# Talking-heads attention and a feed-forward layer: score tiles of 8 heads x 16 queries, and feed-forward work queued between the chunks of the next batch

## The chip, the cores and the metric

The kernel runs on one core of one Trainium2 chip. The metric is the device time of one execution in microseconds (us). "PE" is TensorE's matmul stream, "PEld" its weight loads, DVE is VectorE, ACT ScalarE, POOL GpSimd. PSUM is the memory that matmuls write, in eight banks that this kernel gives out through pools.

## The reference, cut to what matters

There are 8 batches of 12 heads, 448 positions and 64 columns a head. All inputs are float32, and the kernel computes in bfloat16 with float32 accumulation.

```python
scores = (1 / 8) * (q @ k.transpose(0, 1, 3, 2))            # [8, 12, 448, 448]
scores = einsum('bhij,hg->bgij', scores, w_pre)              # mix the heads
attn   = softmax(scores, axis=-1)
attn   = einsum('bhij,hg->bgij', attn, w_post)               # mix them again
x      = (attn @ v) as 3584 rows of 768
out    = maximum(x @ w_in, 0) ** 2 @ w_out                   # 768 -> 2048 -> 768
```

Mixing heads is a matmul over the partition axis if the partitions of a score tile hold (head, query) pairs. One tile holds 128 of the 12 x 448 pairs.

## The kernel before

A batch is 14 chunks of 32 queries. A chunk has three score tiles, each of 4 heads x 32 queries, made by two 64-column matmuls (two heads each). Every output tile of the first mixing needs all three, so mixing is 3 x 3 matmuls of 448 columns. The second mixing and the transposition of the weights come together: the normalised tile is the stationary operand and a matrix built from `w_post` is the moving one, 4 row blocks x 3 matmuls of 384 columns.

```python
for b in range(B):
    ...                                                   # cut: loads of batch b + 1
    for c in range(NCH + 1):
        if c < NCH:
            for t in range(3):                            # scores, 2 x 64 columns
                s_ps = psA.tile(...)
                for x in range(2):
                    nc.tensor.matmul(s_ps[64*x:64*x+64, 0:S], lhsT=ql[2*t+x][:, c, :], rhs=kt[2*t+x], ...)
                # copied to bfloat16 by ScalarE (t < 2) or VectorE
            for gqo in range(3):                          # mixing: 3 x 3 matmuls
                for t in range(3):
                    nc.tensor.matmul(m_ps, lhsT=wpre_cat[t][:, gqo*128:(gqo+1)*128], rhs=S_t[t], ...)
                nc.scalar.activation(e_sb, m_ps, Exp, scale=SCALE, accum_out=sm)
                nc.vector.reciprocal(rc, sm)
                nc.vector.tensor_scalar(d_sb, e_sb, rc, 1.0 / S, mult, subtract)
        if c >= 1:
            for jb in range(4):                           # second mixing, 4 x 3 matmuls
                for t in range(3):
                    nc.tensor.matmul(at_ps[0:jsize, 0:384], lhsT=Dprev[t][:, 128*jb:...], rhs=wpost_cat[t], ...)
                nc.vector.tensor_copy(atb[jb][0:jsize, :, C32(c - 1)], at_ps[0:jsize, 0:384])
    # the mean that was subtracted comes back as a bias: column sums of v, by matmuls
    # ot = v.T @ at, then the first feed-forward (16 x 6 matmuls), transposes of batch b + 1,
    # the second feed-forward (8 blocks x 16 matmuls)                    # cut
```

The softmax here doesn't subtract the row's maximum and nothing guards it: scores larger than these inputs give would overflow.

Of the kernel before, what the change touches and what calls it, by code (L numbers as in the profile page):

```python
# [9 lines left out]
F32 = mybir.dt.float32  # L11

B, H, S, D = 8, 12, 448, 64
DMODEL = H * D
DFF = 2048
CH = 32
NCH = S // CH
ST = [128, 128, 128, 64]
NST = 4
NPAIR = H // 2  # L20
NQ = H // 4
FT = DFF // 128
SCALE = 1.0 / 8.0
ACT = mybir.ActivationFunctionType
ALU = mybir.AluOpType


def C32(cc):
    return slice(cc * CH, (cc + 1) * CH)


@with_exitstack
def kernel(
# [18 lines left out]
    qlp = ctx.enter_context(tc.tile_pool(name="qlp", bufs=1))  # L52
    atbp = ctx.enter_context(tc.tile_pool(name="atbp", bufs=1))
    ffnp = ctx.enter_context(tc.tile_pool(name="ffnp", bufs=1))
    psA = ctx.enter_context(tc.tile_pool(name="psA", bufs=5, space=bass.MemoryType.PSUM))
    psB = ctx.enter_context(tc.tile_pool(name="psB", bufs=3, space=bass.MemoryType.PSUM))
# [3 lines left out]
    istripe = consts.tile([P, 32], BF16, name="istripe")  # L60
    nc.vector.tensor_add(out=istripe[:, :], in0=ident[:, 0:32], in1=ident[:, 32:64])
    nc.vector.tensor_add(out=istripe[:, :], in0=istripe[:, :], in1=ident[:, 64:96])
    nc.vector.tensor_add(out=istripe[:, :], in0=istripe[:, :], in1=ident[:, 96:128])
    onescol = consts.tile([P, 1], BF16, name="onescol")
    nc.vector.memset(onescol[:, :], 1.0)
    onescol_f = consts.tile([P, 1], F32, name="onescol_f")
    nc.vector.memset(onescol_f[:, :], 1.0)
# [3 lines left out]
    wcol_pre = []  # L71
    wcol_post = []
    for t in range(NQ):
        wpre_t = consts.tile([P, H], F32, name=f"wcolpre{t}")
        wpost_t = consts.tile([P, H], F32, name=f"wcolpost{t}")
        for hq in range(4):
            h = 4 * t + hq
            src_pre = bass.AP(tensor=w_pre.tensor, offset=w_pre[h, 0:1].offset, ap=[[0, 32], [1, H]])
            nc.sync.dma_start(out=wpre_t[32 * hq:32 * hq + 32, 0:H], in_=src_pre)
            src_post = bass.AP(tensor=w_post.tensor, offset=w_post[h, 0:1].offset, ap=[[0, 32], [1, H]])  # L80
            nc.sync.dma_start(out=wpost_t[32 * hq:32 * hq + 32, 0:H], in_=src_post)
        wcol_pre.append(wpre_t)
        wcol_post.append(wpost_t)

    wpre_cat = []
    wpost_cat = []
    for t in range(NQ):
        a_t = consts.tile([P, H * 32], BF16, name=f"wprecat{t}")
        b_t = consts.tile([P, H * 32], BF16, name=f"wpostcat{t}")
        for g in range(H):  # L90
            nc.vector.tensor_scalar_mul(out=a_t[:, g * 32:(g + 1) * 32], in0=istripe[:, :], scalar1=wcol_pre[t][:, g:g + 1])
            nc.vector.tensor_scalar_mul(out=b_t[:, g * 32:(g + 1) * 32], in0=istripe[:, :], scalar1=wcol_post[t][:, g:g + 1])
        wpre_cat.append(a_t)
        wpost_cat.append(b_t)
# [3 lines left out]
    cg_ps = psB.tile([P, 384], F32, name="cg_ps", tag="psB")  # L98
    nc.tensor.matmul(cg_ps[0:64, 0:H], lhsT=onesblk[0:H, 0:64], rhs=wpost_bf[0:H, 0:H], start=True, stop=True)
    nc.tensor.matmul(cg_ps[64:128, 0:H], lhsT=onesblk[0:H, 0:64], rhs=wpost_bf[0:H, 0:H], start=True, stop=True)  # L100
    cg2 = consts.tile([P, H], F32, name="cg2")
    nc.vector.tensor_scalar_mul(out=cg2[:, 0:H], in0=cg_ps[:, 0:H], scalar1=1.0 / S)
    cgblk = consts.tile([P, NPAIR], F32, name="cgblk")
    for c2 in range(NPAIR):
        nc.vector.tensor_copy(out=cgblk[0:64, c2:c2 + 1], in_=cg2[0:64, 2 * c2:2 * c2 + 1])
        nc.vector.tensor_copy(out=cgblk[64:128, c2:c2 + 1], in_=cg2[64:128, 2 * c2 + 1:2 * c2 + 2])

    ql = []
    for p in range(NPAIR):
        ql_p = qlp.tile([P, NCH, 64], BF16, name=f"ql{p}", tag=f"ql{p}", bufs=1)  # L110
        nc.vector.memset(ql_p[:, :, :].rearrange("p a b -> p (a b)"), 0.0)
        ql.append(ql_p)

    w1 = []
    w2 = []

    def emit_w1_loads():
        for c2 in range(NPAIR):
            w1_c = wts.tile([P, DFF], BF16, name=f"w1_{c2}")
            nc.gpsimd.dma_start(out=w1_c[:, :], in_=moe_w_in[c2 * 128:(c2 + 1) * 128, 0:DFF])  # L120
            w1.append(w1_c)

    def emit_w2_loads():
        for ft in range(FT):
            w2_f = wts.tile([P, DMODEL], BF16, name=f"w2_{ft}")
            nc.gpsimd.dma_start(out=w2_f[:, :], in_=moe_w_out[ft * 128:(ft + 1) * 128, 0:DMODEL])
            w2.append(w2_f)

    def load_stage(b):
        qs = []  # L130
        ks = []
        vs = []
        for st in range(NST):
            nrows = ST[st]
            s0 = 128 * st
            qst = stage.tile([P, H, D], BF16, name="qst", tag="qst", bufs=8)
            nc.gpsimd.dma_start(out=qst[0:nrows, :, :], in_=q[b, :, s0:s0 + nrows, :].rearrange("h s d -> s h d"))
            qs.append(qst)
            kst = stage.tile([P, H, D], BF16, name="kst", tag="kst", bufs=8)
            nc.gpsimd.dma_start(out=kst[0:nrows, :, :], in_=k[b, :, s0:s0 + nrows, :].rearrange("h s d -> s h d"))  # L140
            ks.append(kst)
            vst = stage.tile([P, H, D], BF16, name="vst", tag="vst", bufs=8)
            nc.gpsimd.dma_start(out=vst[0:nrows, :, :], in_=v[b, :, s0:s0 + nrows, :].rearrange("h s d -> s h d"))  # L143
            if st == NST - 1:
                nc.vector.memset(vst[64:128, :, :].rearrange("p h d -> p (h d)"), 0.0)
            vs.append(vst)
        return qs, ks, vs

    def emit_prologue(qs, ks):
        qt = []  # L150
        kt = []
        for p in range(NPAIR):
            qt_ps = psA.tile([P, S], BF16, name="qt_ps", tag="psA")
            for st in range(NST):
                nrows = ST[st]
                src2d = qs[st][0:nrows, :, :].rearrange("s h d -> s (h d)")
                nc.tensor.transpose(qt_ps[:, 128 * st:128 * st + nrows], src2d[:, p * 128:(p + 1) * 128], ident[0:nrows, 0:nrows])  # L157
            qt_p = work.tile([P, S], BF16, name="qt_p", tag="qt", bufs=6)
            nc.vector.tensor_copy(out=qt_p[:, :], in_=qt_ps[:, :])
            qt.append(qt_p)  # L160
            kt_ps = psA.tile([P, S], BF16, name="kt_ps", tag="psA")
            for st in range(NST):
                nrows = ST[st]
                src2d = ks[st][0:nrows, :, :].rearrange("s h d -> s (h d)")
                nc.tensor.transpose(kt_ps[:, 128 * st:128 * st + nrows], src2d[:, p * 128:(p + 1) * 128], ident[0:nrows, 0:nrows])  # L165
            kt_p = work.tile([P, S], BF16, name="kt_p", tag="kt", bufs=6)
            nc.scalar.copy(out=kt_p[:, :], in_=kt_ps[:, :])
            kt.append(kt_p)
            nc.vector.tensor_copy(out=ql[p][0:64, :, 0:32], in_=qt_p[0:64, 0:S])
            nc.vector.tensor_copy(out=ql[p][64:128, :, 32:64], in_=qt_p[64:128, 0:S])  # L170
        return qt, kt

    staged = {}
    staged[0] = load_stage(0)
    emit_w1_loads()
    staged[1] = load_stage(1)
    emit_w2_loads()
    prologued = {}
    prologued[0] = emit_prologue(staged[0][0], staged[0][1])

    for b in range(B):
        qs, ks, vs = staged[b]
        qt, kt = prologued[b]

        if 1 <= b and b + 1 < B:
            staged[b + 1] = load_stage(b + 1)

        atb = []
        for jb in range(NST):
            t_ = atbp.tile([P, H, S], BF16, name=f"atb{jb}", tag=f"atb{jb}", bufs=1)  # L190
            atb.append(t_)
        nc.gpsimd.memset(atb[NST - 1][64:128, :, :].rearrange("p h d -> p (h d)"), 0.0)

        Dprev = None
        for c in range(NCH + 1):
            if c < NCH:
                S_t = []
                for t in range(NQ):
                    s_ps = psA.tile([P, S], F32, name="s_ps", tag="psA")
                    for x in range(2):  # L200
                        p = 2 * t + x
                        nc.tensor.matmul(  # L202
                            s_ps[64 * x:64 * x + 64, 0:S],
                            lhsT=ql[p][:, c, :],
                            rhs=kt[p][:, 0:S],
                            start=True,
                            stop=True,
                        )
                    s_sb = work.tile([P, S], BF16, name="s_sb", tag="S", bufs=6)
                    if t < 2:  # L210
                        nc.scalar.copy(out=s_sb[:, :], in_=s_ps[:, :])  # L211
                    else:
# [42 lines left out]
            if c < NCH:  # L255
                Dprev = Dcur
# [98 lines left out]
```

## Time and profile before

The median of two runs was 981.12 us (980.83 to 981.42).

These are lines of the page of the kernel before: the span; busy time, share of the span and instructions of each engine; the granted TensorE clock in 40 slices, in tenths; and the chain of work that ended last, by engine.

```profile
span 979.9 us, 15128 instructions
PE 935.6 (95%) x5698; PEld 486.8 (50%) x5698; DVE 594.5 (61%) x1633; ACT 456.3 (47%) x1185; POOL 141.9 (14%) x133
PEclk9999999999999999999999999999999999999999
PE 88%; DVE 6%; ACT 4%; DMA 1%; issue 1%; SPq 1%; ACTq 0%; DVEq 0%
```

PE is busy in 95% of the span at its full clock, and the chain runs through PE for 88%. So time is saved by taking work from TensorE, not from another engine.

One batch of the kernel before in windows (each row a stretch of time, with the busy time of each engine in it, the granted clock and the DMA engines' share): chunks; bias and products with v; first feed-forward; second feed-forward with the transposes of q and k.

```profile
core 0: us, PE busy (x) PEld busy (x) DVE busy (x) ACT busy (x) POOL busy (x), PEclk, DMA share, GB/s
268.10:335.90 67.80, 65.42 (x383) 31.99 (x381) 53.67 (x153) 38.10 (x113) 0.00 (x0) 1.00 0.01 3
335.90:343.20 7.30, 7.30 (x64) 3.60 (x61) 2.13 (x5) 2.72 (x5) 0.00 (x0) 1.00 0.01 2
343.20:361.40 18.20, 18.20 (x99) 9.39 (x97) 9.39 (x16) 8.91 (x17) 8.40 (x5) 1.00 0.60 39
361.40:386.80 25.40, 25.40 (x175) 15.68 (x174) 6.96 (x20) 7.08 (x14) 7.62 (x8) 1.00 0.99 102
```

The 118.7 us of a batch are 67.8 us of chunks (14 of 4.84) and 50.9 us of the rest; PE is nearly full in each row.

Matmuls overlap, so a duration (0.35 us) is not a cost. The cost is the distance to the next start: 189 ns for 448 columns, 162 ns for 384.

### The profile page before, as it was taken

The page shows a single profiled execution, that of the slowest core. Times are in us where ns is not written, and L with a number is a line of the kernel's source. Part 1 is how long each engine was busy: PE and PEld are TensorE (multiplying, and loading weights), DVE is VectorE, ACT ScalarE, POOL GpSimd, SP SyncE. Part 2 cuts the span into 40 slices and gives each one's busy share as a digit, 9 for nine tenths or more (in the row PEclk, how much of TensorE's full clock was granted, in tenths as well). Part 3 has the DMA queues.
Part 4 walks back from the last instruction along what each step waited for, and adds up shares of the span by engine and source line. Part 5 has one row for each costly group of instructions (what it writes and reads, how often), then busy time and mean ns, then how long its engine had stood idle before and what let it go on. Part 6 is the DMA issues. An engine that isn't in the chain of part 4 may idle for free.

```text
span 979.9 us, 15128 instructions
## 1 busy us (share of the span) xinstructions
PE 935.6 (95%) x5698; PEld 486.8 (50%) x5698; DVE 594.5 (61%) x1633; ACT 456.3 (47%) x1185; POOL 141.9 (14%) x133
## 2 busy tenths in 40 slices
PE   2999999999999999999999999999999999999998
PEld 1444565445644455444554445544455444554455
DVE  7788436874178661886628855388544884358840
ACT  1555425545265452554435544355434554355441
POOL 7570330003300032001410023000300001000000
PEclk9999999999999999999999999999999999999999
DMA  9990490004900049001580045500400000100001
GB/s 133 181 171 2 29 106 9 1 1 29 109 5 1 1 29 113 1 1 8 37 98 1 1 27 44 73 1 1 29 29 28 1 1 2 41 17 1 1 1 57
DMA packets 143177, 34.83 MB, mean 36 GB/s; under 512 B 133120, under 2 KB 142336, under 8 KB 143104
## 3 DMA queue, kind: packets, MB, share of 16 engines
q0 software_dynamic: 133760, 22.81, 29.9%
q1 hardware_dynamic: 9344, 11.05, 3.5%
q8 instruction: 44, 0.72, 0.3%
q14 instruction: 29, 0.24, 0.1%
HBM read 45.65 MB, written 11.01 MB: 58 GB/s over the span
## 4 chain that ended last, share of the span: by engine, by line
PE 88%; DVE 6%; ACT 4%; DMA 1%; issue 1%; SPq 1%; ACTq 0%; DVEq 0%
PE m_ps L219 20%; PE at_ps L247 19%; PE o_ps L314 17%; PE h_ps L293 15%; PE s_ps L202 7%; PE ot_ps L278 4%; ACT e_sb L228 3%; PE kt_ps L165 2%; DVE d_sb L232 2%; PE qt_ps L157 2%; PE colsum_ps L264 1%; ACT s_sb L211 1%; DVE rc L230 1%; DMA wcolpost_108<-in_w_post_dram 1%; DMA wcolpost_118<-in_w_post_dram 0%
## 5 line engine op out<-in xcount | busy, mean ns | idle before, releaser
L228 ACT ACTIVATE e_sb<-m_ps 128x448 f32<-128x448 f32 x336 | 181.0, 542 | 172.5 <-PE m_ps L219 148.4
L247 PEld LDWEIGHTS <-d_sb 128*128 128x128 bf16 (+1 forms) x1344 | 127.7, 100 | 154.6 <-DVE d_sb L232 46.1
L247 PE MATMUL at_ps<-wpostcat_128,d_sb 128*128 128x384 bf16 x448 | 146.2, 330 | 14.5 <-DVE d_sb L232 5.8
L213 DVE CAST s_sb<-s_ps 128x448 bf16<-128x448 f32 x112 | 67.7, 605 | 137.5 <-PE s_ps L202 137.5
L232 DVE TENSOR_SCALAR d_sb<-e_sb,rc 128x448 bf16<-128x448 f32 x336 | 144.3, 453 | 1.5
L247 PE MATMUL at_ps<-wpostcat_154,d_sb 128*128 128x384 bf16 x448 | 144.6, 326 | 0.4 <-DVE d_sb L232 0.2
L211 ACT CAST s_sb<-s_ps 128x448 bf16<-128x448 f32 x224 | 116.4, 532 | 43.3 <-PE s_ps L202 24.8
L247 PE MATMUL at_ps<-wpostcat_180,d_sb 128*128 128x384 bf16 x448 | 131.1, 326 | 0.1
L301 ACT ACTIVATE hr<-h_ps 128x448 f32<-128x448 f32 x128 | 69.7, 544 | 75.7 <-PE h_ps L293 75.7
L143 POOL DMA_DIRECT2D vst<-in_v_dram x32 | 30.8, 972 | 481.4 <-PE ot_ps L278 478.0
L219 PE MATMUL m_ps<-s_sb,wprecat_127 128*128 128x448 bf16 x336 | 94.8, 354 | 5.8 <-ACT s_sb L211 5.5
L322 ACT COPY osb<-o_ps 128x384 f32<-128x384 f32 (+1 forms) x64 | 30.6, 477 | 136.3 <-PE o_ps L314 93.6
L219 PE MATMUL m_ps<-s_sb,wprecat_153 128*128 128x448 bf16 x336 | 93.0, 354 | 0.0
L219 PE MATMUL m_ps<-s_sb,wprecat_179 128*128 128x448 bf16 x336 | 87.7, 354 | 0.3 <-DVE s_sb L213 0.3
L230 DVE RECIPROCAL rc<-sm 128x1 f32<-128x1 f32 x336 | 52.6, 157 | 33.9 <-ACT e_sb L228 26.6
L228 ACT ACTIVATION_READ_ACCUMULATOR e_sb<-m_ps 128x1 f32 x336 | 66.7, 199 | 0.0
L286 ACT ACTIVATE xt_c<-ot_ps,bvec 128x448 bf16<-128x448 f32 x48 | 27.7, 634 | 57.4 <-DVE bvec L270 56.4
L219 PEld LDWEIGHTS <-wprecat_127 128*128 128x128 bf16 x336 | 30.0, 97 | 42.8 <-issue 29.4
L219 PEld LDWEIGHTS <-wprecat_153 128*128 128x128 bf16 x336 | 32.8, 98 | 29.4 <-issue 0.8
L219 PEld LDWEIGHTS <-wprecat_179 128*128 128x128 bf16 x336 | 33.0, 98 | 28.3 <-issue 1.2
L293 PE MATMUL h_ps<-xt_c,w_0_262 128*128 128x448 bf16 x128 | 45.2, 353 | 0.0
L293 PE MATMUL h_ps<-xt_c,w_3_268 128*128 128x448 bf16 x128 | 45.1, 352 | 0.0
(561 smaller groups left out, 1794.7 us busy)
## 6 DMA issues: line engine op xcount, KB each, us to landing
out_dram<-osb SPq DMA_DIRECT2D x48, 192.0 KB, 1.9
qst<-in_q_dram POOLq DMA_DIRECT2D x24, 192.0 KB, 6.1
kst<-in_k_dram POOLq DMA_DIRECT2D x24, 192.0 KB, 6.6
vst<-in_v_dram POOLq DMA_DIRECT2D x24, 192.0 KB, 5.2
out_dram<-osb SPq DMA_DIRECT2D x16, 96.0 KB, 2.1
qst<-in_q_dram POOLq DMA_DIRECT2D x8, 96.0 KB, 7.5
kst<-in_k_dram POOLq DMA_DIRECT2D x8, 96.0 KB, 7.9
vst<-in_v_dram POOLq DMA_DIRECT2D x8, 96.0 KB, 5.4
```

The costliest lines, as they stand in the source:

```text
L202: nc.tensor.matmul(s_ps[64 * x:64 * x + 64, 0:S], lhsT=ql[p][:, c, :], rhs=kt[p][:, 0:S], start=True, stop=True,)
L211: nc.scalar.copy(out=s_sb[:, :], in_=s_ps[:, :])
L213: nc.vector.tensor_copy(out=s_sb[:, :], in_=s_ps[:, :])
L219: nc.tensor.matmul(m_ps[:, 0:S], lhsT=wpre_cat[t][:, gqo * 128:(gqo + 1) * 128], rhs=S_t[t][:, 0:S], start=(t == 0), stop=(t == NQ - 1),)
L228: nc.scalar.activation(out=e_sb[:, :], in_=m_ps[:, :], func=ACT.Exp, scale=SCALE, accum_out=sm[:, 0:1])
L230: nc.vector.reciprocal(out=rc[:, 0:1], in_=sm[:, 0:1])
L232: nc.vector.tensor_scalar(out=d_sb[:, :], in0=e_sb[:, :], scalar1=rc[:, 0:1], scalar2=1.0 / S, op0=ALU.mult, op1=ALU.subtract,)
L247: nc.tensor.matmul(at_ps[0:jsize, 0:384], lhsT=Dprev[t][:, 128 * jb:128 * jb + jsize], rhs=wpost_cat[t][:, 0:384], start=(t == 0), stop=(t ...
L278: nc.tensor.matmul(ot_ps[64 * hh:64 * hh + 64, 0:S], lhsT=vs[jb][:, g, :], rhs=atb[jb][:, g, :], start=(jb == 0), stop=(jb == NST - 1),)
L293: nc.tensor.matmul(h_ps[:, 0:S], lhsT=w1[c2][:, ft * 128:(ft + 1) * 128], rhs=xt[c2][:, 0:S], start=(c2 == 0), stop=(c2 == NPAIR - 1),)
L301: nc.scalar.activation(out=hr[:, :], in_=h_ps[:, :], func=ACT.Relu)
L314: nc.tensor.matmul(o_ps[0:msize, 0:384], lhsT=h2t[ft][:, mt * 128:mt * 128 + msize], rhs=w2[ft][:, nt * 384:(nt + 1) * 384], start=(ft == ...
```

## The change

Its intent is to make the mixing denser. A score tile now holds 8 heads x 16 queries (two tiles for heads 0 to 7), and a third tile holds heads 8 to 11 of both query groups. The first two output tiles then need two matmuls each; the third needs one full matmul and two half ones of 64 columns that can run side by side. Scores are made by 32-column matmuls, four to a tile. In the second mixing, a 384-column matmul and two of 192 do what three of 384 did, and the last 64 rows of both tiles share a PSUM tile. The bias takes 24 one-column matmuls. The last 64 rows of the second feed-forward are made for both halves at once. Squares move from VectorE to GpSimd. And the products with v, the feed-forward and the next transposes go into a list of units, from which each chunk takes some.

```diff
+    def chunk_scores(b, c):
+        for t in range(3):
+            for r in range(4):                      # four 32-column matmuls a tile
+                p, n = (r, 2*c + t) if t < 2 else (4 + r % 2, 2*c + r // 2)
+                nc.tensor.matmul(ps[32*r:32*r+32, 0:S], lhsT=ql[b % 2][p][:, n, :], rhs=kt[p][:, 0:S], ...)
+    def chunk_mix(b, c):
-            for t in range(NQ): nc.tensor.matmul(m_ps, lhsT=wpre_cat[t][...], rhs=S_t[t], ...)   # 3 x 3
+        for u, A in enumerate((A0, A1)):
+            nc.tensor.matmul(ps[:, 0:S], lhsT=preA[:, 0:128], rhs=A, ...)
+            nc.tensor.matmul(ps[:, 0:S], lhsT=preBA[u], rhs=Bt, ...)
+        nc.tensor.matmul(ps[:, 0:S], lhsT=preBB, rhs=Bt, ...)
+        for u, A in enumerate((A0, A1)):
+            nc.tensor.matmul(ps[64*u:64*u+64, 0:S], lhsT=preA[:, 128:192], rhs=A, ...)
+    def chunk_post(b, c):
+        for jb in range(3):
+            nc.tensor.matmul(ps[:, 0:384], lhsT=dB[:, js], rhs=postBB, ...)
+            nc.tensor.matmul(ps[:, 0:192], lhsT=d0[:, js], rhs=postA, ...)
+            nc.tensor.matmul(ps[:, 192:384], lhsT=d1[:, js], rhs=postA, ...)
+        # last 64 rows: four 64-column matmuls of 192
...                                                 # cut: loads, constants, bias, ot, feed-forward units
+    def run_filler(ns):
+        while filler and ns > 0:
+            w, f = filler.pop(0)
+            f()
+            ns -= w
+        return ns
+    for s in range(len(steps) + 2):
+        chunk_scores(step s); chunk_mix(step s - 1); chunk_post(step s - 2)
+        # appended where due: ot_units, ffn_units, bias_unit; at the front: prologue_units
+        debt = run_filler(3200 + debt)
```

PSUM goes from pools of 5 and 3 banks to four pools of 2. In the start, the zero fills of the query tiles move from VectorE to GpSimd.

A slot is the 0.19 us from one matmul of 448 columns to the next. A mode switch is a change between output tiles of 32, 64 and 128 columns. The order in which TensorE gets its matmuls is not that of the source: a scheduler makes it when the kernel is built, and "the built order" is its result.

## The prediction

> **What bounds it now.** TensorE. The page shows PE busy 95% at a granted clock of 1.0, and the chain that ended last is 88% PE. The timeline splits a batch of 118.7 us into 67.8 us of chunks (14 of 4.84 us), 7.3 us of bias and attention-times-V, 18.2 us of first and 20.4 us of second feed-forward matmuls, 4.9 us of transposes; 27 us precede the first chunk. By starts of consecutive matmuls, 448 columns cost 189 ns and 384 cost 163 ns; 64-column output tiles run two at a time (second start about 10 ns later). Going from 128- to 64-column matmuls or back costs 285 instead of 189 ns: about 95 ns per switch. The Trainium skill (TensorEngine Tiling (Array Packing), Key Properties) says that changing the tiling mode drains TensorE; this trace agrees. Per chunk VectorE works 3.9 us, ScalarE 3.3.
>
> **What the change does per chunk.** Mixing falls from 9 to 6 slots of 189 ns, post-mixing from 12 x 163 ns to 3 x 327 plus about 165. Scores stay 3 slots only if four 32-column tiles run together; the skill (same page, Theoretical Speedup) gives "up to 4x", no trace here shows it. Without mode switches that is 2.8 us. But the built program's order has about ten switches per chunk (32 / 128 / 64 columns interleaved; a score tile is also split, costing a slot) against two to four before. I sum 3.2 us streaming + 0.95 us switching = 4.17 us, against 4.84 measured. VectorE loses one 0.54 us eviction but keeps a cast (0.60), three evictions (0.55), three normalisations (0.41), one reciprocal: 3.7 us. ScalarE gains an eviction: two casts (0.53), three exps (0.74 with accumulator read), about 0.35: 3.6 us. Walking one period by hand through the waits (third mixing tile, exp, reciprocal, normalisation, post-mixing, next third mixing tile) gives about 4.3 us; with slack 4.45.
>
> **What it does not do.** The diff issues feed-forward between chunks. In the built order each batch's 96 + 96 + 32 feed-forward matmuls stand in one unbroken block after its chunks. So chunks still run without filler, and the overlap gains nothing. What gains is the last 64 rows of the second feed-forward, two halves together (about 2.6 us per batch), and the bias (24 tiny matmuls for 8 of 384 columns). Squares move to GpSimd: estimated from the skill (GPSIMD Engine Reference, Elementwise side-by-side) at 2.6 cycles an element, about 1 us, just under the 1.13 us of a unit, so roughly hidden.
>
> **Sum.** Batch: chunks 62, transposes 5 to 6, bias 2, attention-times-V 6, feed-forward 37 to 38: about 113 us, against 118.7. Start about 22 us (V no longer sits between Q and K loads). Total about 920 us, range 885 to 960. Chances: faster by over 2% 0.89, within 2% 0.08, slower 0.03.
>
> **What would show it.** Timeline: unbroken feed-forward of 36 to 38 us per batch; chunk period 4.2 to 4.7 us; score matmuls in groups of four starting within some 10 ns of each other; switches near 95 ns. PE stays the chain's main engine; GpSimd squares near 1 us.
>
> **What would make it wrong.** Four score tiles not running together (+1 us a chunk or more: no gain or slower). A switch to 32 columns costing more than 95 ns. GpSimd squares far over 1.13 us, holding up feed-forward. Evictions with 16-element runs slower than 0.55 us. On the other side, tile queues overlapping across segments: near 4.0 us a chunk, 880 us.

## More of the kernel before

A round is up to four 32-column score matmuls side by side.

## The result, and the profile after

The median was 917.03 us (916.87 to 917.19, two runs), ratio 0.9342 with a 95% interval of 0.9315 to 0.9369. A ratio here is the mean time of one kernel's runs over that of the other's runs in the same rounds, so it is not quite the ratio of the medians quoted. The change is faster by 6.6%, and 3 us from the prediction.

The same lines of the page, after:

```profile
span 915.4 us, 17324 instructions
PE 872.0 (95%) x6914; PEld 434.1 (47%) x6914; DVE 429.8 (47%) x1070; ACT 502.3 (55%) x1337; POOL 241.9 (26%) x277
PEclk9999999999999999999999999999999999999999
PE 5%; DVE 0%; ACT 0%; issue 0%; ACTq 0%
```

PE is as full as before with 64 us less work. The chain of waits is of no use here: it breaks off after 5% of the span, so its shares say nothing about what limited the rest. The windows do. A batch between feed-forward blocks, then the feed-forward block:

```profile
162.70:234.40 71.70, 71.07 (x642) 33.44 (x640) 51.20 (x125) 50.78 (x145) 7.83 (x8) 1.00 0.33 23
234.40:270.90 36.50, 36.46 (x224) 20.52 (x224) 0.00 (x0) 11.95 (x23) 19.14 (x21) 1.00 0.43 55
```

A batch takes 108.2 us, 10.5 less than before: 7.3 in the chunks (14 of 4.32 instead of 4.84), 2.6 in the last rows of the second feed-forward (b_tail below), the rest elsewhere. In the second row VectorE does nothing at all for 36.5 us, and PE's 224 instructions are the 96 + 96 + 32 feed-forward matmuls: the block is unbroken, nothing was interleaved.

Part of one chunk on PE in the timeline of the changed kernel (start, length, engine and line, operation, tiles, shapes as rows*columns of the stationary operand):

```profile
439.10 0.25 PE L354 MATMUL at_ps<-postA,d_sb 128*128 128x192 bf16 x1
439.28 0.36 PE L300 MATMUL s_ps<-kt_p,ql_1_185 128*32 128x448 bf16 x1
439.28 0.36 PE L300 MATMUL s_ps<-kt_p,ql_2_187 128*32 128x448 bf16 x1
439.29 0.36 PE L300 MATMUL s_ps<-kt_p,ql_3_189 128*32 128x448 bf16 x1
439.29 0.36 PE L300 MATMUL s_ps<-kt_p,ql_0_183 128*32 128x448 bf16 x1
439.48 0.35 PE L300 MATMUL s_ps<-kt_p,ql_1_185 128*32 128x448 bf16 x1
...
439.77 0.36 PE L321 MATMUL m_ps<-s_sb,preA 128*128 128x448 bf16 x1
439.97 0.33 PE L352 MATMUL at_ps<-postBB,d_sb 128*128 128x384 bf16 x1
...
441.66 0.35 PE L322 MATMUL m_ps<-s_sb,preBA_174 128*128 128x448 bf16 x1
441.94 0.36 PE L300 MATMUL s_ps<-kt_p,ql_0_183 128*32 128x448 bf16 x1
442.24 0.34 PE L352 MATMUL at_ps<-postBB,d_sb 128*128 128x384 bf16 x1
```

Three things are to be seen. Four 32-column matmuls start within 0.01 us and the next round begins 0.19 us later, so four together cost what one does. Going from 32 to 128 columns costs 0.29 us (439.48 to 439.77) where a round costs 0.19. And at 441.94 a single 32-column matmul stands alone between two mode switches: the built order splits score tiles, so that a chunk has ten switches and five score rounds, where three rounds would do. The period is 4.32 us. In all of it each start follows the one before by what the matmul streams, or by that and up to 0.12 us where the mode changes: there is no wait on TensorE.

The spans of the two profiled runs differ by 64.5 us. By the starts of the batches' first feed-forward matmuls, the first stands at 126.2 us instead of 106.0 (+20.2), the seven batch intervals are 748.3 instead of 831.1 (-82.8), and what follows the last start is 40.9 instead of 42.8 (-1.9). The first chunk starts at 33.9 us instead of 27.0. Much of the rest of the 20.2 is order and not loss: the first chunks of the next batch (first score at 108.6 us) now stand before a batch's feed-forward, where they stood after it. Why the start is late is seen in three views of the changed kernel's first microseconds: GpSimd, VectorE and PE.

```profile
9.08 0.94 POOL L138 MEMSET ql_0_183<- 128x896 bf16 x1
...
18.05 0.93 POOL L138 MEMSET ql_5_205<- 128x896 bf16 x1
...
22.07 0.53 POOL L153 DMA_DIRECT2D wpost_bf<-in_w_post_dram  x1
```

```profile
10.37 8.65 DVE L100 CAST istripe<-ident 128x16 f32<-128x16 bf16 x1 [8.97 <-POOL ident masks.py:199]
```

```profile
23.75 0.16 PE L155 MATMUL cg_ps<-wpost_bf,onesblk 12*64 12x12 bf16 x1 [23.75 <-DVE preB L118]
```

A VectorE cast of 16 elements a partition took 8.65 us, ending as GpSimd's twelve fills of the query tiles did; and the load of `w_post`, which GpSimd issues, stood behind all fills at 22.07 us, and PE's first matmul needs it.

### The profile page after: what moved, and what is told of

Its sections match the earlier page's. It is cut to its first block, busy times and chain, and to the rows that moved or that the text cites. A ratio compares the mean times of both kernels' runs of the same rounds, so it can differ in the third digit from the quotient of the medians.

```text
span 915.4 us, 17324 instructions
## 1 busy us (share of the span) xinstructions
PE 872.0 (95%) x6914; PEld 434.1 (47%) x6914; DVE 429.8 (47%) x1070; ACT 502.3 (55%) x1337; POOL 241.9 (26%) x277
## 5 line engine op out<-in xcount | busy, mean ns | idle before, releaser
L357 DVE CAST at<-at_ps 128x384 bf16<-128x384 f32 x336 | 181.1, 550 | 394.0 <-PE at_ps L354 389.3
L304 ACT CAST s_sb<-s_ps 128x448 bf16<-128x448 f32 x224 | 115.8, 534 | 37.2 <-PE s_ps L300 36.5
L352 PE MATMUL at_ps<-postBB,d_sb 128*128 128x384 bf16 x336 | 111.0, 330 | 1.5 <-DVE d_sb L335 0.7
L73 POOL DMA_DIRECT2D qst<-in_q_dram x32 | 31.8, 993 | 275.7 <-PE qt_ps L190 223.9
L353 PE MATMUL at_ps<-postA,d_sb 128*128 128x192 bf16 x336 | 83.2, 248 | 0.0
L354 PE MATMUL at_ps<-postA,d_sb 128*128 128x192 bf16 x336 | 82.7, 246 | 0.0
L321 PE MATMUL m_ps<-s_sb,preA 128*128 128x448 bf16 x224 | 81.0, 362 | 0.0
L264 ACT COPY osb<-o_ps 128x384 f32<-128x384 f32 x48 | 23.0, 478 | 101.2 <-PE o_ps L262 101.2
L242 ACT ACTIVATE xt<-ot_ps,bvec 128x224 bf16<-128x224 f32 x96 | 40.1, 447 | 23.3 <-PE ot_ps L237 23.1
L352 PEld LDWEIGHTS <-d_sb 128*128 128x128 bf16 x336 | 32.6, 97 | 40.2 <-issue 28.6
L248 PE MATMUL h_ps<-xt,w_0_272 128*128 128x448 bf16 x128 | 45.1, 352 | 1.2 <-ACT xt L242 0.5
L327 PE MATMUL m_ps<-s_sb,preA 128*64 128x448 bf16 x224 | 45.4, 378 | 0.0
L248 PE MATMUL h_ps<-xt,w_5_282 128*128 128x448 bf16 x128 | 45.1, 352 | 0.0
L248 PE MATMUL h_ps<-xt,w_4_280 128*128 128x448 bf16 x128 | 45.1, 352 | 0.0
L248 PE MATMUL h_ps<-xt,w_3_278 128*128 128x448 bf16 x128 | 45.1, 352 | 0.0
L248 PE MATMUL h_ps<-xt,w_2_276 128*128 128x448 bf16 x128 | 45.1, 352 | 0.0
L248 PE MATMUL h_ps<-xt,w_1_274 128*128 128x448 bf16 x128 | 45.1, 352 | 0.0
```

Of the source, the lines that this page charges most:

```text
L248: nc.tensor.matmul(ps[:, 0:S], lhsT=w1[c2][:, ft * 128:(ft + 1) * 128], rhs=xts[(b, c2)][:, :], start=(c2 == 0), stop=(c2 == NPAIR - 1))
L304: nc.scalar.copy(out=sb[:, :], in_=ps[:, :])
L321: nc.tensor.matmul(ps[:, 0:S], lhsT=preA[:, 0:128], rhs=A[:, :], start=True, stop=False)
L327: nc.tensor.matmul(ps[64 * u:64 * u + 64, 0:S], lhsT=preA[:, 128:192], rhs=A[:, :], start=False, stop=True, skip_group_check=True)
L352: nc.tensor.matmul(ps[:, 0:384], lhsT=dB[:, js], rhs=postBB[:, :], start=True, stop=False, skip_group_check=True)
L353: nc.tensor.matmul(ps[:, 0:192], lhsT=d0[:, js], rhs=postA[:, :], start=False, stop=True, skip_group_check=True)
```

## The experiments

Twelve kernels ran, each with three rounds against the kernel before, all with correct results. The two theories were: **A**, TensorE's streaming plus its switches set the time, so that what counts is the number of slots, switches and waits on TensorE; **B**, the interleaving or the loop through exp and normalisation sets it. The mean time from one batch's first score matmul to the next one's (batches 1 to 7) is the best single number of each, as it leaves out start and end.

| kernel | us | ratio to before | us a batch | first score, us |
|---|---|---|---|---|
| before | 981.1 | | 118.71 | 27.0 |
| changed | 917.0 | 0.934 | 108.24 | 33.9 |
| b_tail | 961.0 | 0.978 | 116.08 | 26.6 |
| e_memset | 909.1 | 0.926 | 108.24 | 19.5 |
| e_slots | 974.7 | 0.993 | 116.00 | 33.9 |
| e_square | 917.4 | 0.933 | 108.29 | 33.8 |
| e_nocredit | 878.3 | 0.894 | 102.52 | 33.9 |
| e_combo | 870.4 | 0.886 | 102.51 | 19.7 |
| e_order | 961.5 | 0.978 | 113.69 | 41.0 |
| e_mix | 943.8 | 0.960 | 112.49 | 33.9 |
| e_fix | 870.9 | 0.886 | 100.38 | 33.8 |
| e_fix7 | 849.2 | 0.864 | 98.19 | 31.5 |
| e_start | 856.3 | 0.871 | 98.24 | 36.5 |
| e_best | 841.4 | 0.856 | 95.68 | 37.5 |

### b_tail: one part of the change alone

The kernel before, with only the last 64 rows of the second feed-forward made for both halves at once.

```diff
-        for mt in range(NST):
+        for mt in range(3):
...
+        for ft in range(FT):
+            for n2 in range(2):
+                nc.tensor.matmul(o_ps[64*n2:64*n2+64, 0:384], lhsT=h2t[ft][:, 384:448],
+                                 rhs=w2[ft][:, n2*384:(n2+1)*384], ...)
```

> The kernel before with one part of the change alone: the last 64 rows of the second feed-forward run as two 64-column tiles side by side. It removes 16 of 128 slots of 163 ns per batch: 2.6 us, less about 0.2 us for switching the mode, so 8 x 2.4 = 19 us: about 962 us (ratio 0.980). If two such tiles did not run together, 981 us.

It took 961.0 us (ratio 0.9783, 0.9757 to 0.9809). A batch became 2.63 us shorter: 16 of 32 slots of 162 ns are 2.6 us. So about 20 of the change's 64 us come from these lines, which have nothing to do with the mixing.

### e_slots: more TensorE work in the chunk

The changed kernel with three more 448-column matmuls a chunk, whose weights are zero.

```diff
+            nc.tensor.matmul(ps[:, 0:S], lhsT=zero[:, :], rhs=A[:, :], start=False, stop=True)    # twice
+        nc.tensor.matmul(ps[:, 0:S], lhsT=zero[:, :], rhs=Bt[:, :], start=False, stop=False, ...)  # once
```

> The changed kernel with three matmuls of zero weights added to the mixing of each chunk (same result; mixing back to 9 slots of 189 ns, as in the kernel before). The built order shifts too: about 4 score slots in place of 5 and 9 switches in place of 10, which gives back about 0.28 us of the 0.57 us. Theory A (TensorE binds the chunk): the chunk period rises from 4.32 to about 4.6 us, the total to about 945 to 950 us. Rival B (the loop through exp and normalisation binds, TensorE waits in it): the chunk period stays near 4.32 us and the total within 1% of 917 us.

It took 974.7 us, more than either theory said. The steady chunk takes 4.80 us, 0.48 more. The built order has a round and a switch fewer (four and nine), as expected, so of the 0.57 us of the three slots 0.28 are given back and TensorE has 0.28 us more to do. The other 0.2 us is a wait, on two lines of PE's timeline:

```profile
446.71 0.33 PE L357 MATMUL at_ps<-postBB,d_sb 128*128 128x384 bf16 x1
447.08 0.35 PE L329 MATMUL m_ps<-s_sb,preBB 128*128 128x448 bf16 x1
```

The third mixing tile starts 0.37 us after a 384-column matmul that is followed in 0.16 elsewhere. ScalarE's exp of the first mixing tile, which holds one of the pool's two banks, lasts until 446.9. So the added work was not hidden, which speaks against B. But the loop through exp does cost a wait in this order, and a batch's 7.76 us, 0.554 a chunk, are near three slots of 0.189 by chance. That the changed kernel's own chunk has no slack on TensorE rests on its starts, shown above, and on e_order below.

### e_square: the squares back on VectorE

```diff
-        nc.gpsimd.tensor_tensor(out=h2[:, :], in0=hr[:, :], in1=hr[:, :], op=ALU.mult)
+        nc.vector.tensor_tensor(out=h2[:, :], in0=hr[:, :], in1=hr[:, :], op=ALU.mult)
```

> The changed kernel with the squares of the feed-forward given back to VectorE; nothing else. In the changed kernel GpSimd takes 0.95 us a square and the first feed-forward product 18.1 us a batch, 1.13 us for each square, so the move to GpSimd neither binds nor gains: 917 us within 3 (theory A). Theory B (the move relieves VectorE and is part of the gain): 5 us or more slower. Theory C (GpSimd's squares disturb VectorE's copies beside them): 5 us or more faster.

917.4 us, no change: which engine squares is of no weight here. In the changed kernel a square takes GpSimd 0.95 us. The estimate from the Trainium skill ("GPSIMD Engine Reference", 3.1 Elementwise: about 2.6 cycles an element at 1.2 GHz) is 0.97 us for 448 elements, and this trace agrees.

### e_memset: the start

The changed kernel with its zero fills back on VectorE.

```diff
-            nc.gpsimd.memset(t[:, :, :].rearrange("p a b -> p (a b)"), 0.0)
+            nc.vector.memset(t[:, :, :].rearrange("p a b -> p (a b)"), 0.0)     # and those of vlast
```

> The changed kernel with the sixteen zeroing memsets at the start moved from GpSimd to VectorE. Theory: in the changed kernel a 128x16 cast on VectorE lasted 8.65 us while GpSimd ran these memsets, and a small load that TensorE's first instruction needs was issued behind them; so the first chunk comes 7 to 10 us earlier (33.9 to about 25) and the total falls to about 908 to 910 us. Rival: the loads of Q and K set the start, no change (917 us).

909.1 us, as expected; the batches are the same and the first score stands at 19.5 us (about 25 were expected). The cast that had taken 8.65 us, in VectorE's timeline of this run:

```profile
16.49 0.17 DVE L100 CAST istripe<-ident 128x16 f32<-128x16 bf16 x1
```

The first score is 14 us earlier, and the time 8: the rest of the gain is given back in the first chunk, where PE waits once for 6.8 us, up to 27.8 us, until VectorE has copied earlier transposes. The Trainium skill ("GPSIMD Engine Reference", 1. Specifications) says that GpSimd shares its SBUF interfaces with VectorE, with contention for VectorE instructions of a two-port mode or with two SBUF inputs. The 8.65 against 0.17 us fit that; the cast reads one tile, so it can only be of the first kind, but no run here shows its mode. But seven additions right after it, beside later fills, read two tiles each and took 1.43 us together from 19.06 us on, no more each than three without fills beside them in e_memset (0.59 us): beside fills, which only write, the second kind was not slowed.

### e_nocredit: really between the chunks

The built order shows one block of feed-forward, but not why. The source does: `debt` is what `run_filler` leaves over. With an empty list, all 3200 ns are left and are carried over. Fourteen steps bank 44,800 ns, and the products with v, the transposes and the bias are listed with 9,240 of them; what is over, with what the first batch left, is about the 36,280 that a whole feed-forward is listed with. When it is listed, it is issued at once. One line ends it:

```diff
-        debt = run_filler(3200 + debt)
+        debt = min(0, run_filler(3200 + debt))
```

> The changed kernel with one line altered: time that the feed-forward queue leaves unused in a chunk is no longer carried over as credit (the queue was empty for most of a batch, so that by the time the feed-forward is queued the whole of it is issued at once). In the built order the feed-forward matmuls now stand between the chunks, each chunk has about 8 tiling-mode switches in place of 10 to 11 and 3 score slots in place of 5. Theory A (chunks are bound by TensorE, of which mode switches and split score tiles are a quarter): the period of a batch falls from 108.3 us by about 14 x 0.6 = 8 to 10 us, the total to about 850 to 860 us. Rival B (the chunk period of 4.32 us is set by the loop of mixing, exp, normalisation and post-mixing): filling the waits with feed-forward hides nearly all of the 36.5 us feed-forward block, the batch falls to about 65 to 75 us and the total under 700 us. Rival C (the block against interleaving makes no difference): 917 us.

878.3 us (ratio 0.8943, 0.8922 to 0.8963): 38.7 us better than the change, short of A's 850 to 860 and far from B's under 700. A batch falls from 108.24 to 102.52 us, so interleaving does pay. But not by filling idle time, for PE was full: in a window of 100 us it was busy for 99.3 before this edit and for 99.6 after. A step with three first-product units takes 7.18 us; less their 18 x 0.189 us that leaves 3.78 us for the chunk, where the changed kernel needs 4.32. In those steps the chunk has eight switches and three score rounds instead of ten and five: with other work at hand, score tiles are no longer split. The gain came through the order on TensorE.

### e_combo: do the two gains add?

e_nocredit and e_memset together.

> The changed kernel with both single edits already measured, e_nocredit (878.3 us) and e_memset (909.1 us, 8.0 us less than the change). If the start and the batches' middle are independent, as theory A says: 870.4 us, within 2. If the 8 us at the start are only moved to a later wait once the batches are shorter: 876 to 879 us.

870.42 us against 870.4 from adding. Start and batches are independent.

### e_order: a fixed order in the chunk

The chunk's functions are cut into pieces, and TensorE keeps the order of the source: two score tiles, two mixing tiles, the third score tile, two blocks, the third mixing tile, the last blocks.

```diff
+    pe_order = ctx.enter_context(tc.manual_schedule(engines={mybir.EngineType.PE}))
-            chunk_scores(b, c); chunk_mix(*steps[s - 1]); chunk_post(*steps[s - 2])
+            score_tile(b, c, 0); score_tile(b, c, 1)
+            mix_head(*steps[s - 1], 0); mix_head(*steps[s - 1], 1)
+            score_tile(b, c, 2)
+            post_block(*steps[s - 2], 0); post_block(*steps[s - 2], 1)
+            mix_last_a(*steps[s - 1]); mix_last_b(*steps[s - 1])
+            post_last(*steps[s - 2]); post_block(*steps[s - 2], 2)
```

> The changed kernel with TensorE's order within a chunk fixed: two score tiles (8 matmuls of 32 columns), the first two mixing tiles, the third score tile, two at blocks, the third mixing tile, the last at block. That is 6 mode switches and 3 rounds of score matmuls a chunk, where the changed kernel's own order has 10 switches and 5 rounds. The feed-forward stays one block. Theory A (a chunk is TensorE streaming plus switching): 4 x 0.095 us and 2 x 0.189 us less, 0.76 us of 4.32, so at best 3.56 us a chunk and 832 us; as a fixed order will now and then wait, about 3.9 us and 870 us are expected. Theory B (a chunk's length is set by the loop through exp, sum, reciprocal and subtraction): the period stays 4.3 us and the time 912 to 920 us.

961.5 us: a miss by 90 us. The chunk itself did as A said in direction, 3.80 us instead of 4.32. But the batch got longer, 113.69 us. Two of its stretches in the windows, the transposes of q and k and what follows:

```profile
422.00:430.00 8.00, 5.90 (x52) 3.41 (x49) 6.42 (x18) 4.22 (x12) 0.00 (x0) 1.00 0.01 2
430.00:438.50 8.50, 6.96 (x47) 3.26 (x46) 3.00 (x9) 4.06 (x10) 4.23 (x5) 0.60 0.47 30
```

And three lines of PE's timeline there:

```profile
427.98 0.46 PE L201 MATMUL kt_ps<-ident,kst 128*128 128x128 bf16 x4 [0.69 <-DVE ql L194]
...
431.83 0.64 PE L190 MATMUL qt_ps<-ident,qst 128*128 128x128 bf16 x4 [0.62 <-ACT kt_p L204]
...
434.86 0.94 PE L298 MATMUL s_ps<-kt_p,ql 128*32 128x448 bf16 x8
```

With the order fixed, all 12 groups of four transposes stand one after the other and wait for two PSUM banks to be copied out, some 0.6 us at a time. In the changed kernel the scheduler hid most of these waits under chunks: beyond its feed-forward (36.5 us) and 14 steady chunks, a batch takes 11.3 us there and 24.0 here. The second loss is the column before the last two of the windows, the granted clock: after 8 us at 74% busy it fell to 0.60 on average over the next window, the same four transposes take 0.64 us instead of 0.46, and eight score matmuls 0.94 us (0.56 at full clock, in e_mix). The Trainium skill ("TensorE: Matmul & The Clock Gate", Part 1) puts the fall to half the clock after an idle window of about 3.4 us. The same part also tells of a kernel that cycles through PSUM banks, whose short idle times between groups of matmuls were enough to make the clock fall again and again. This trace agrees with the second account: the longest idle time of PE before the fall was 0.69 us. The transposes alone do not do it: the kernel before makes its 48 in 5.1 us (361.5 to 366.6) without waiting, at a clock of 1.00. How much waiting it takes, no run here shows.

### e_mix: fixed order, interleaving and start at once

e_order, with e_memset and with the feed-forward spread as in e_nocredit (3400 ns a step, after the last block, so next to 128-column work); products with v and bias go to the front of the list.

> The fixed order of e_order, plus the feed-forward really spread over the next batch's chunks (no credit carried over; 3400 ns a step, always after the last at block, so that it adds no switch), plus the zero fills moved from GpSimd to VectorE. Theory A (everything that is left is TensorE's sum of streaming and switches): a batch of about 97 us where e_nocredit had 101.9, and 8 us less at the start: 825 to 845 us. Theory B (the three gains are the same time counted three times, or the pinned order stalls): 865 us or more.

943.8 us: a miss as well. A batch is 112.49 us, and the mean clock 0.961. The steady step with three units takes 7.21 us, so the chunk 3.81 us: the fixed order's six switches gave nothing over the 3.78 us of e_nocredit with eight. Two switches were saved, but leaving the 64-column matmuls, now four in a row after the two of the mixing, costs 355 ns instead of 178, for a reason that no run here shows. Besides, the transposes again wait in a row, and the products with v wait up to 1.8 us for the copies just before them.

### e_fix: the waits taken out

e_mix, with two groups of transposes in each of six steps instead of 12 groups in a row (the expectation counts 24 by mistake), feed-forward units between them, and the products with v one step later. The budget is 3100 ns a step, and the bias and the 64-column unit of the feed-forward move too (not shown).

```diff
-            if pc == CPH - 1: filler[0:0] = ot_units(pb, 0)
+            if pc == CPH - 1: split.extend(ot_units(pb, 0))          # issued in the next step
-        if s < len(steps) and c == 7 and b + 1 < B: filler[0:0] = prologue_units(b + 1)
+        if live and 7 <= c < 13 and b + 1 < B: small.extend(pro[2*(c-7):2*(c-7)+2])
```

> e_mix with its stalls taken out, the order within a chunk as before. In e_mix all 24 groups of transposes of a batch stood together and waited for two PSUM buffers, about 0.85 us a group, in which the granted clock fell to half; and the products with V stood right after the last at block, 1.7 to 2.0 us before its copies. Here two groups of transposes stand in each of six steps, with feed-forward work between them, and the products with V come a step later. Theory A (stalls and the clock they cost are what e_mix lost): no drop of the granted clock, a batch of 97 to 99 us, 840 to 855 us, so faster than e_combo (870.4). Theory B (fixing TensorE's order costs by itself, in many short waits): 870 us or more.

870.9 us: 73 us better than e_mix, with a clock of 0.997, so the stalls and their clock were what e_mix lost. But a batch is 100.38 us, not 97 to 99, and the total is level with e_combo's 870.4. The order of e_fix is better by 2 us a batch, and its first score stands 14 us later. Theory B's bound (870 or more) was met just as well; by total time alone this run doesn't decide, by batch time it is A with too high a hope.

### e_fix7: fewer switches for the transposes

The last 64 rows of q and of k share one tile of 128 rows. A head pair then takes 7 transposes of 128 rows, and not 6 of 128 and 2 of 64; key rows stand in another order, the same for k and v.

```diff
-            for st in range(4): nc.tensor.transpose(ps[:, 128*st:128*st+n], qs[st][0:n, ...], ident[0:n, 0:n])
+            for j in range(7): nc.tensor.transpose(ps[:, j, :], srcs[j][:, 2*p:2*p+2, :]..., ident[:, :])
```

> e_fix, with the last 64 rows of q and of k staged in one tile of 128 rows, so that the q and k of two heads take 7 transposes of 128 rows instead of 6 of 128 and 2 of 64: up to 24 mode switches fewer on each side of a batch, and half as many groups. The key rows stand in another order, the same for k and v. Theory A: 24 to 48 switches of 0.095 us less a batch, 2 to 4 us, so 815 to 840 us if e_fix is 840 to 855. Rival: the switches to 64-row transposes cost nothing and the result is within 5 us of e_fix.

849.2 us (ratio 0.8643). 21.7 us less than e_fix, far outside the rival's 5 us. TensorE's switches over the whole run fell from 840 to 675. A batch fell by 2.19 us, the low end of A's 2 to 4; A's total of 815 to 840 us had counted on a faster e_fix. Not all of it is switches: there are also half as many groups that wait for a bank.

### e_start: a start that did not get earlier

e_fix7, with the two small products with `w_post` behind the first transposes, and `w_post` loaded in float32 by another queue and cast by VectorE.

```diff
-    nc.gpsimd.dma_start(out=wpost_bf[:, :], in_=w_post[0:H, 0:H])              # before the transposes
+    nc.sync.dma_start(out=wpost_f[:, :], in_=w_post[0:H, 0:H])                 # after them
+    nc.vector.tensor_copy(out=wpost_bf[:, :], in_=wpost_f[:, :])
```

> e_fix7 with the two small products with w_post, which TensorE takes first, moved behind the first transposes, and w_post loaded through another queue than GpSimd's. In e_fix7 (849.2 us) the first score product stands at 31.5 us, as everything on TensorE is fixed behind these two; in e_combo, where they wait less, at 19.7 us. Theory A (the start is serial with the rest): 8 to 12 us less, 837 to 841 us. Rival (the first batch then waits for the loads of the second instead): 845 to 850 us.

856.3 us, 7 us slower, where A had 8 to 12 us less and the rival no change. VectorE's waits in the first 37 us name the reason:

```profile
DVE wpost_bf L393 <- DMA wpost_f<-in_w_post_dram: 10.8, 1, 10.8
```

The new cast stands early in VectorE's order and waits 10.8 us for its load, and everything else on VectorE waits behind it: the constants, and the copies of the transposes, for which TensorE then waits. The wait was moved to an engine with more work behind it. A start with a better order on VectorE was not tried.

### e_best: transposes behind the feed-forward of a step

e_start, with the step's feed-forward units first and its transposes last.

```diff
+        ns -= sum(w for w, _ in small)
+        while ns > 0 and ffn: ...                   # feed-forward units first
+        for w, f in small: f()                      # then transposes and bias
```

> e_start with the transposes of a step placed behind the step's feed-forward work instead of before and between it. In e_fix7 some five times a batch a feed-forward product waits 1.04 us, where it follows its own predecessor in 0.19 us elsewhere, because the transposes before it hold one of two PSUM buffers until VectorE and ScalarE have copied them. Theory A: 0.86 us x 5 x 7 batches, 30 us less than e_start at most; 20 to 30 us expected, so about 812 to 822 us. Rival (the wait moves to the next step's score tiles, whose copies the same engines make): within 8 us of e_start.

841.4 us (ratio 0.8561, 0.854 to 0.8582), 14.9 us less than e_start: short of A's 20 to 30, beyond the rival's 8. PE's waits in one batch, first e_fix7:

```profile
PE h_ps L240 <- ACT hr L244: 2.8, 4, 0.7
PE ot_ps L226 <- ACT xt L234: 0.5, 3, 0.2
```

then e_best:

```profile
PE ot_ps L214 <- ACT xt L222: 0.5, 2, 0.3
PE qk_ps L181 <- DVE bvec L203: 0.3, 1, 0.3
```

The four waits before a feed-forward product are gone, 2.8 us; a batch fell by 2.56. The view names the engine: the product waited for the ReLU of the one before, since with one of two banks held by the transposes only one was left for the feed-forward. This is the fastest version run. Compared by medians of different rounds, it takes 0.918 of the changed kernel's time. It still starts late, with its first score at 37.5 us against e_combo's 19.7.

## Why the prediction was right, point by point

- **TensorE bounds it: right.** PE is busy 95% before and after, the changed kernel's chunk has no wait on PE, and e_order made it 0.52 us shorter by fixing TensorE's order.
- **Four 32-column matmuls run together: right.** They start within 0.01 us, 0.19 us a round. The Trainium skill ("TensorEngine Tiling (Array Packing)", Theoretical Speedup) says up to four times; here all of it is reached, for these shapes.
- **About 95 ns a switch: right** in the form that was predicted, 0.28 to 0.31 us instead of 0.19. The skill's drain at a change of mode (same page, Key Properties) is what is seen; the page gives no length.
- **Chunk of 4.45 us: nearly right.** It is 4.32; the walk by hand gave 4.3, and the slack that was added for safety was not there. But the walk's agreement with the period was chance: in e_order the same dependences, with no other work between the chunks, fit in 3.80 us. Streaming and switching set the 4.32, not the waits (the prediction's sum of the two was 4.17).
- **The feed-forward stays one block: right**, 36.5 us against 37 to 38. "The overlap gains nothing" was right too, but the prediction read it off the built order and did not say why; the credit of `run_filler` is why.
- **Batch of about 113 us: too long by 5.** The mis-sized terms: 2 us for a bias whose one-column matmuls start every 25 ns, so 0.6 us for all 24; chunks 62 for 60.5; feed-forward 37 to 38 for 36.5; products with v and transposes 11 to 12 us for about 11, the bias included. Chunks and bias count most. The skill has the figure: "TensorE: Matmul & The Clock Gate", Part 1, gives a floor of about 25 ns from start to start, and this trace agrees. "TensorEngine Tiling (Array Packing)", Instruction Overhead, says that one column takes as long as 60, with some 60 cycles a matmul; at the 2.4 GHz of the first page that is the same 25 ns.
- **Start of about 22 us: wrong, it is 33.9.** The step that failed is "V no longer sits between Q and K loads": it looked at loads alone. The wait was for GpSimd's fills, which held up a VectorE cast for 8.65 us and the load of `w_post` to 22.07 us. e_memset moved the fills and the first score came at 19.5 us.
- **The PE share of the chain** can't be checked: the chain of the changed kernel breaks off after 5%.

So the total was hit to within 3 us because errors cancel. The prediction's terms are 22 us and eight batches of 113, of which the last has no transposes to make (5 to 6 us): 920. Against that, the six steady batch intervals were 4.8 us shorter each, 29 in all; the start was 12 us later; and the first and last batch together took about 12 us more, which no run here takes apart. The direction and the size rest on sound terms, the last 3 us on luck.

## What to carry to other kernels

On a full TensorE, count switches of the tiling mode and rounds of side-by-side tiles as carefully as columns; interleaving other work can pay by letting the order be better even where there is no idle time to fill. When work is handed out by budget, check that an empty list doesn't bank its budget, and look at the built order to see whether the interleaving is there at all. Fixing an engine's order by hand takes away the scheduler's hiding of waits too: spread whatever waits for a buffer, put it before a stretch that doesn't need that buffer, and look at the granted clock.

## What the Trainium skill lacked or had wrong

- "TensorEngine Tiling (Array Packing)", Key Properties, has the drain at a change of mode but no length: here 0.28 to 0.31 us from start to start instead of 0.19 for 448 columns between 128 and 32 or 64 columns, some 90 to 120 ns more; 355 instead of 178 ns when leaving four 64-column matmuls that follow two others, not explained.
- "TensorE: Matmul & The Clock Gate", Part 1, has the fall of the clock by short idle times, but no length or share of them: in e_order it fell after 8 us at 74% busy, with no idle time over 0.69 us before the fall.
- "GPSIMD Engine Reference", 1. Specifications, names the shared interfaces; no page gives what a row of GpSimd instructions costs one VectorE instruction: a cast of 16 elements a partition took 8.65 us beside GpSimd's fills of 0.93 us each, and 0.17 us without.
